# Delta rule and Prelu feed-forward on one core: slopes moved into ScalarE's scale, matmul fillers between the stages of the first chain, conversions dealt out anew

## The chip, the cores and the metric

The kernel runs on one core of a Trainium2 chip. The metric is the device time of one execution in microseconds (us): 669.74, the median of three runs. A core has five engines that run beside each other and meet through semaphores: TensorE (PE, matrix products into the banks of PSUM), VectorE (DVE) and ScalarE (ACT) (elementwise work), GpSimd (POOL), and SyncE (SP), which here issues nearly all the DMA transfers.

## The reference

Two blocks one after the other. The first is the delta rule over 768 time steps for 4 x 8 heads of size 48; the second multiplies the result, as 3072 tokens of 384 numbers, by w_in (384 x 2048), applies a Prelu with a slope per column, and multiplies by w_out (2048 x 384).

```python
k_n = k / (np.linalg.norm(k, axis=-1, keepdims=True) + 1e-06)
for t in range(S):
    kt, vt, bt = (k_n[:, :, t], v[:, :, t], beta[:, :, t, None])
    y[:, :, t] = np.einsum('bhd,bhde->bhe', q[:, :, t], state)
    v_old = np.einsum('bhde,bhd->bhe', state, kt)
    state = state + bt[:, :, :, None] * np.einsum('bhd,bhe->bhde', kt, vt - v_old)
x = y.transpose(0, 2, 1, 3).reshape(B * S, H * D)
h = x @ w_in
g = np.maximum(h, 0.0) + alpha * np.minimum(h, 0.0)
return g @ w_out
```

All data are fp32. alpha lies between 0 and 0.3.

## The kernel before

**Tiling.** Time is cut into 12 chunks of 64 steps (C); a step n of the kernel is one chunk of one pair of batches, so there are 24. Inside a chunk the recurrence becomes triangular algebra: the products of the keys (`grams`, L416) are weighted by beta and the norms (`weigh`, L350), a triangular matrix of 64 x 64 for each head is inverted, first in blocks of 32 (`eliminate`, L499, a long chain of pairs of DVE instructions L514 and L520 with a POOL instruction L504 ahead of it), and the blocks are joined by small products: `between_1` and `between_2` (L671 on PE, with the copies L686 on ACT after each) and `placing` (L624), which puts the inverted blocks, times a mask, into the tile inv. Then `through_state` (L731), `solve` (L762: L765 on PE, L769 on DVE makes u), `outputs` (L774: L778 on PE) and `next_state` (L788: L794 on PE, L802 on DVE) give the chunk's result y and the new state, and `to_ffn` (L810) transposes y on PE (L817) and copies it to xt (L819, ACT) as input of the second block.

**The second block.** `ffn_in` (L899), used for the first 8 chunks, makes 8 pairs of products: for each pair 6 matmuls (L908) fill one of two PSUM banks p_ffn; ACT (L918) writes max(-h, 0) of both halves to SBUF, and DVE adds it, times 1 - alpha, to h (L920, once for each half, as the slope is a number per partition). The bank is free for the next pair but one after L920. `ffn_in_fast` (L1094), for the last 4 chunks, does the same from SBUF: `total` (L1169, DVE), `below` (L1175, ACT), `slope` (L1179, DVE, twice). Their places in time are numbers of PE's steps, kept in a list of due times. `ffn_out` (L938) and its fast forms multiply by w_out.

**Weights.** The two weight matrices come by DMA into staging tiles and are converted, tile by tile, by two ACT instructions (L225, L226) and two DVE instructions (L235, L240): `weights` (L182). One part of a conversion is one of the two DVE instructions; ACT's two are issued up to two tiles ahead. w_in has 12 tiles (24 parts), staged in the space that w_out will take, six at a time: tile 7 can be fetched when tile 1 is converted, and the first w_out tiles that are staged there (four transfers in SP's queue) when the last w_in tiles are. The transfers stand in SP's queue in the order of the program.

**Order of the work.** It is written out by hand; each engine executes its instructions in the order in which the program issues them. `first_chunk` (L1394) is the chain of steps 0 and 1, at the start, when there is no other work for PE. The elimination of its blocks runs on DVE while PE does `busy(BUSY)` (L1531): matmuls of the identity that nobody reads, 512 columns each, here called fillers (L1368; `busy(0.5)` is one of 256 columns). There are two more fillers in the chain, of 0.75 and 0.5. In `first_chunk` the copies and placings of step 1 are on DVE (the arguments `vector` and `by_vector`, L684 and L635), those of step 0 mostly on ACT. 12 parts of the conversion are issued in it, all after `outputs(1)`.

`second_pair` (L1551) does steps 2 and 3 and weaves into them the first chunk's `ffn_in`: `alongside(products, pieces)` issues so many matmuls and so many parts of conversion between two stages. In it the products are dealt out as 4, 5, 4, 4, 5, 5, 5, 5, 5 and the rest, the parts as 2, 2, 2, 2, 3, 3, 3, 2, 2, 1. After it, `ffn_in(1)`, the rest of the conversion, `statics` and the elimination for steps 4 to 7 are woven together (L1622), and from then on attention, elimination and feed-forward run beside each other to the end.

**PSUM.** Three pairs of banks (p_pair) are handed out in turn by `ps_big` and `ps_one` (L76, L81); a filler takes a turn.

## Time and profile before

| what | value |
|---|---|
| median of the three runs | 669.74 us (669.43 to 669.76) |
| profiled execution, its own time | 668.25 us |
| its span, first to last instruction | 666.5 us |
| PE busy, weight loads | 642.7 us (96%), 569.2 us (85%) |
| DVE busy | 494.3 us (74%) |
| ACT busy | 263.1 us (39%) |
| POOL busy | 92.1 us (14%) |
| mean granted clock of PE | 0.984 |
| the chain that ended last, by engine | PE 81%, DVE 11%, ACT 3%, issue 2% |

The profile is one execution, recorded by the hardware. It is read in views: a page of totals; groups of instructions by source line, with count, busy time and mean duration in ns, and after the bar the idle time of the engine just ahead of them and what ended it; windows, which give for stretches of time the busy time of each engine (the number of instructions in brackets), the clock that PE was granted (PEclk, 1.00 is full speed), the busy share of the DMA engines and GB/s; and the timeline, with start, duration, engine, line and operation of each run of instructions, and in square brackets the idle time before it with its releaser. "Issue" as a releaser means that the engine waited for nothing that the profile shows. An fp32 matmul shows as two records. PEld is PE's loading of weights, which overlaps with its products. SPq is SP issuing DMA transfers.

### The profile page before, as it was taken

The numbers are of one execution on the slowest core, as the hardware profiler recorded it, in microseconds if no ns is written. First come the engines' busy times: TensorE is split into PE (matmuls) and PEld (weight loads), VectorE is DVE, ScalarE is ACT, GpSimd is POOL, SyncE is SP. The second block draws the span as 40 slices with busy tenths as digits, with TensorE's granted clock in tenths as the row PEclk, the third lists the DMA queues.
The fourth block names the chain that finished last, engine by engine and source line by source line (L and its number), as shares of the span: only waits on it lengthen the run. The fifth ranks groups of instructions, "written<-read, shape, count | busy, mean of one in ns | idle before, by whom it ended". The sixth has DMA issues, their size and how long they took to land.

```text
span 666.5 us, 22092 instructions
## 1 busy us (share of the span) xinstructions
PE 642.7 (96%) x9535; PEld 569.2 (85%) x9535; DVE 494.3 (74%) x1180; ACT 263.1 (39%) x613; POOL 92.1 (14%) x201
## 2 busy tenths in 40 slices
PE   6979999999999999999999999999999999999997
PEld 4567878656687998998998998998999999999997
DVE  4875879868999859758959757858968658568393
ACT  5736855335455343334343333223235235042140
POOL 6000121001010000001000000000035044052250
PEclk9959999999999999999999999999999999999999
DMA  8848844211432032122112112112112210100000
GB/s 126 230 114 218 197 107 120 71 37 27 77 69 49 12 64 49 22 54 49 25 40 36 24 40 37 24 39 37 26 38 38 37 37 4 28 12 1 25 1 25
DMA packets 110962, 37.72 MB, mean 57 GB/s; under 512 B 104160, under 2 KB 107248, under 8 KB 110864
## 3 DMA queue, kind: packets, MB, share of 16 engines
q1 hardware_dynamic: 109088, 35.81, 25.0%
q8 instruction: 75, 1.23, 0.8%
q10 hardware_dynamic: 1776, 0.49, 0.4%
q14 instruction: 23, 0.19, 0.1%
HBM read 31.56 MB, written 4.72 MB: 54 GB/s over the span
## 4 chain that ended last, share of the span: by engine, by line
PE 81%; DVE 11%; ACT 3%; issue 2%; DMA 1%; POOL 1%; SPq 0%; DVEq 0%; POOLq 0%; ACTq 0%
PE p_ffn L908 21%; PE p_ffn L972 17%; PE p_more L1225 8%; PE p_more L1140 4%; PE p_ffn L1130 3%; PE p_ffn L1225 3%; PE p_pair L375 3%; PE p_pair L671 2%; PE p_ffn L1135 2%; PE p_pair L740 2%; PE p_pair L765 2%; PE p_pair L778 2%; DVE prod L514 2%; PE p_pair L422 2%; DVE block L520 2%
## 5 line engine op out<-in xcount | busy, mean ns | idle before, releaser
L908 PE MATMUL p_ffn<-xt,w_in 128*128 128x256 f32 x768 | 176.3, 385 | 3.8 <-ACT sums L918 1.8
L908 PEld LDWEIGHTS p_ffn<-xt,w_in 128*128 128x128 f32 x768 | 143.8, 191 | 24.6 <-ACT sums L918 2.2
L920 DVE SCALAR_TENSOR_TENSOR act<-act,al_t,p_ffn 128x256 f32<-128x256 f32 x112 | 48.6, 475 | 29.0 <-ACT act L918 28.9
L918 ACT ACTIVATE act<-p_ffn 128x512 f32<-128x512 f32 x56 | 33.3, 594 | 80.9 <-PE p_ffn L908 80.7
L520 DVE TENSOR_TENSOR block<-block,prod 128x30 f32<-128x30 f32 (+9 forms) x150 | 49.9, 333 | 5.1
L1164 POOL TENSOR_TENSOR k_t<-k_t 128x128 f32<-128x128 f32 (+1 forms) x48 | 29.2, 608 | 168.0 <-ACT k_t L1159 165.5
L514 DVE TENSOR_TENSOR prod<-block 128x30 f32<-128x30 f32 (+9 forms) x150 | 48.9, 326 | 3.2 <-POOL block L504 1.6
L972 PE MATMUL p_ffn<-w_out,act 128*128 128x192 f32 x288 | 49.6, 329 | 0.1
L972 PEld LDWEIGHTS p_ffn<-w_out,act 128*128 128x128 f32 x288 | 46.5, 190 | 0.8 <-issue 0.5
L819 ACT COPY xt<-p_pair 128x384 f32<-128x384 f32 x22 | 10.4, 478 | 91.3 <-PE p_pair L817 77.5
L364 POOL TENSOR_TENSOR beta_t<-beta_t,rec 128x8 f32<-128x8 f32 x24 | 6.2, 260 | 290.8 <-DVE rec L362 253.8
L1164 POOL TENSOR_TENSOR block<-block 128x128 f32<-128x128 f32 (+1 forms) x48 | 27.3, 569 | 17.1 <-ACT block L1159 14.6
L1130 PE MATMUL p_ffn<-xt,w_in 128*128 128x256 f32 x96 | 28.8, 381 | 0.5 <-DVE o_sb L992 0.5
L686 ACT COPY inv<-p_pair 32x256 f32<-32x256 f32 x46 | 16.6, 361 | 26.9 <-DVE u L769 23.6
L769 DVE TENSOR_TENSOR u<-p_pair,wgt 128x384 f32<-128x384 f32 x24 | 13.2, 555 | 15.5 <-PE p_pair L671 14.8
L1179 DVE SCALAR_TENSOR_TENSOR act<-block,al_t,act 128x256 f32<-128x256 f32 x32 | 20.3, 675 | 5.3 <-ACT block L1175 5.3
L750 DVE TENSOR_TENSOR r<-v_raw,p_pair 64x192 f32<-64x192 f32 (+1 forms) x66 | 23.3, 353 | 1.1
L992 DVE TENSOR_TENSOR o_sb<-u,p_ffn 128x192 f32<-128x192 f32 x24 | 7.9, 352 | 20.2 <-PE p_ffn L972 19.7
L639 ACT ACTIVATE inv<-inverse,which 128x256 f32<-128x256 f32 x45 | 22.0, 504 | 1.7 <-DVE inverse L487 1.4
L1225 PE MATMUL p_more<-w_out,act 128*128 128x192 f32 x128 | 21.9, 330 | 0.0
L1179 DVE SCALAR_TENSOR_TENSOR act<-k_t,al_t,act 128x256 f32<-128x256 f32 x32 | 21.7, 717 | 0.1
L1159 ACT COPY k_t<-p_more 128x512 f32<-128x512 f32 x16 | 9.4, 585 | 31.4 <-PE p_more L1140 26.7
(223 smaller groups left out, 1398.9 us busy)
## 6 DMA issues: line engine op xcount, KB each, us to landing
w_out<-in_moe_w_in_dram SPq DMA_DIRECT2D x12, 512.0 KB, 6.6
qp<-in_q_dram SPq DMA_DIRECT2D x48, 96.0 KB, 3.3
v_raw<-in_v_dram SPq DMA_DIRECT2D x48, 96.0 KB, 3.0
kl<-in_k_dram SPq DMA_DIRECT2D x96, 48.0 KB, 2.6
out_dram<-o_sb SPq DMA_DIRECT2D x92, 48.0 KB, 1.6
space_out<-in_moe_w_out_dram SPq DMA_DIRECT2D x11, 384.0 KB, 5.1
ke<-in_k_dram SPq DMA_DIRECT2D x43, 96.0 KB, 3.5
w_out<-in_moe_w_out_dram SPq DMA_DIRECT2D x5, 384.0 KB, 5.2
```

Source lines behind the costliest of these rows:

```text
L514: nc.vector.tensor_tensor(out=prod, in0=r[:, 0:j, j : j + 1].to_broadcast([128, j, n]), in1=r[:, j : j + 1, j + 1 : HB].to_broadcast([128, ...
L520: nc.vector.tensor_tensor(out=r[:, 0:j, j + 1 : HB], in0=r[:, 0:j, j + 1 : HB], in1=prod, op=ALU.add)
L750: nc.vector.tensor_tensor(out=r[to, a], in0=v_in[to, a], in1=p[own, a, :, 0:D], op=ALU.subtract)
L908: nc.tensor.matmul(p_h[:, i], w_in[:, t, (f + i) * 128 : (f + i + 1) * 128], xt[:, t], start=(t == 0), stop=(t == KT - 1),)
L918: nc.scalar.activation(g, p_h, ACT.Relu, scale=-1.0)
L920: nc.vector.scalar_tensor_tensor(out=g[:, i], in0=g[:, i], scalar=al_t[:, f + i : f + i + 1], in1=p_h[:, i], op0=ALU.mult, op1=ALU.add,)
L972: nc.tensor.matmul(p, x(i), w(i), start=(i == 0), stop=(i == FP - 1))
L1130: nc.tensor.matmul(p[:, f * 256 : f * 256 + 256], w(2, f), xt[:, 2], start=True, stop=False)
L1140: nc.tensor.matmul(q[:, j], a, b, start=True, stop=True)
L1164: nc.gpsimd.tensor_tensor(out=dst, in0=a, in1=b, op=ALU.add)
L1179: nc.vector.scalar_tensor_tensor(out=g[:, f], in0=r[:, f], scalar=al_t[:, 2 * i + f : 2 * i + f + 1], in1=g[:, f], op0=ALU.mult, op1=ALU.add,)
L1225: nc.tensor.matmul(p, x(i), w(i), start=(i == 0), stop=(i == FP - 1))
```

## The change

The slope moves from DVE to ACT. al_t holds alpha - 1 instead of 1 - alpha, and ACT computes max((alpha - 1) h, 0), with al_t as its scale, once for each half, as the scale is a number per partition; DVE adds h to both halves in one instruction. The same in ffn_in_fast.

In `first_chunk`, there is a filler between all stages, `busy` writes to the pair of banks whose turn is next without taking the turn, step 1's copies and its first placing are on ACT, the placings of part 2 and one scaling of v are on POOL, and the conversion's 12 parts are issued in six portions, the first one ahead of `solve`. BUSY is 7 instead of 6. In `second_pair` the parts are dealt out as 1, 1, 1, 1, 3, 3, 3, 3, 3, 3.

```diff
-BUSY = 6
+BUSY = 7
...
-        nc.scalar.activation(al_t, p, ACT.Copy, scale=-1.0, bias=1.0)
+        nc.scalar.activation(al_t, p, ACT.Copy, bias=-1.0)
...
-            if by_vector:
-                nc.vector.tensor_scalar(
+            if by_pool:
+                nc.gpsimd.tensor_scalar(
...
-                if vector:
+                if both and t == 1:
                     nc.vector.tensor_copy(out=to[rows], in_=p[rows])
...
-    def scale_v(n):
+    def scale_v(n, engine=nc.vector):
...
             g = act_of(c, f // 2)
-            nc.scalar.activation(g, p_h, ACT.Relu, scale=-1.0)
             for i in range(2):
-                nc.vector.scalar_tensor_tensor(
-                    out=g[:, i], in0=g[:, i], scalar=al_t[:, f + i : f + i + 1], in1=p_h[:, i],
-                    op0=ALU.mult, op1=ALU.add,
+                nc.scalar.activation(
+                    g[:, i], p_h[:, i], ACT.Relu, scale=al_t[:, f + i : f + i + 1]
                 )
+            nc.vector.tensor_tensor(out=g, in0=g, in1=p_h, op=ALU.add)
...
             def below():
-                h = g.rearrange("p f i -> p (f i)")
-                nc.scalar.activation(r.rearrange("p f i -> p (f i)"), h, ACT.Relu, scale=-1.0)
+                for f in range(2):
+                    nc.scalar.activation(
+                        r[:, f], g[:, f], ACT.Relu, scale=al_t[:, 2 * i + f : 2 * i + f + 1]
+                    )
 
             def slope():
-                for f in range(2):
-                    nc.vector.scalar_tensor_tensor(
-                        out=g[:, f], in0=r[:, f], scalar=al_t[:, 2 * i + f : 2 * i + f + 1],
-                        in1=g[:, f], op0=ALU.mult, op1=ALU.add,
-                    )
+                nc.vector.tensor_tensor(out=g, in0=r, in1=g, op=ALU.add)
...
-        p = ps_one() if p is None else p
+        p = big[0][:, 0] if p is None else p
...
-        busy(0.75)
+        busy(1)
...
+        busy(0.5)
         for b in range(bs):
             for i in range(4):
                 nc.tensor.matmul(
                     two[quad(i), b], half_way[quad(i), b], inverse[0][quad(i), b, LB:HB]
                 )
+            if b == H - 1:
+                busy(0.5)
         scale_v(0)
...
+        now(between_1(0))
+        place(0, (1,))
+        busy(1)
+        now(between_1(1))
+        place(1, (1,))
+        busy(0.5)
         for i in both:
-            now(between_1(i, vector=i == 1))
-            place(i, (1,), True)
-        place(0, (2,))
-        place(1, (2,), True)
-        scale_v(1)
-        for i in both:
-            now(between_2(i, vector=i == 1))
+            place(i, (2,), True)
+        scale_v(1, nc.gpsimd)
+        now(between_2(0))
         mask(0)
-        for i in both:
-            now(through_state(i))
-            now(solve(i))
+        convert(2)
+        busy(1)
+        now(between_2(1))
         mask(1)
-        busy(0.5)
+        now(through_state(0))
+        now(solve(0))
+        convert(2)
+        busy(0.75)
+        now(through_state(1))
+        now(solve(1))
+        convert(2)
         now(outputs(0))
+        busy(1)
         state_of = [next_state(0)]
         to_ffn(0, ps_ffn())
         now(outputs(1))
+        busy(0.5)
         state_of.append(next_state(1))
-        convert(4)
         to_ffn(1, ps_ffn())
         convert(2)
         for i in both:
             now(state_of[i])
             load_late(i + 2)
             load_v(i + 3)
-        convert(4)
+        convert(2)
...
-        alongside(4, 2)
+        alongside(4, 1)
...
-        alongside(5, 2)
+        alongside(5, 1)
...
-        alongside(5, 2)
+        alongside(5, 3)
...
-        alongside(IN_PARTS - 42, 1)
+        alongside(IN_PARTS - 42, 3)
```

## The prediction, put on record before the changed kernel was run

> **What bounds the kernel now.** I read the windows by stage first, then the clock in windows of half a microsecond, the timeline of the start and of 48 to 105 us, the groups with shapes kept apart, and the order of the instructions of both kernels.
>
> ```profile
> core 0: us, PE busy (x) PEld busy (x) DVE busy (x) ACT busy (x) POOL busy (x), PEclk, DMA share, GB/s
> 27.00:33.00 6.00, 4.91 (x315) 3.75 (x314) 4.94 (x11) 2.31 (x4) 0.00 (x0) 1.00 0.42 74
> 33.00:48.80 15.80, 12.36 (x350) 10.32 (x338) 10.65 (x25) 3.87 (x10) 0.00 (x0) 0.57 0.42 105
> 48.80:100.00 51.20, 47.79 (x1050) 40.40 (x1050) 37.87 (x93) 36.86 (x85) 8.41 (x20) 0.97 0.71 175
> 100.00:146.00 46.00, 44.42 (x292) 31.23 (x292) 38.87 (x111) 19.10 (x42) 3.10 (x8) 1.00 0.31 78
> ...
> 240.00:490.00 250.00, 249.46 (x3613) 228.92 (x3612) 189.04 (x469) 83.03 (x202) 6.58 (x18) 1.00 0.20 38
> 490.00:580.00 90.00, 90.00 (x1411) 86.30 (x1410) 63.13 (x118) 35.88 (x81) 27.90 (x48) 1.00 0.13 25
> ```
>
> From 240 to 580 us PE stands still for 0.54 us. Nothing done to ACT or DVE there can pay; only the start and the stages to about 190 us can move the end. The clock is 0.57 in the first chain (33 to 48.8):
>
> ```profile
> 34.50:35.00 0.50, 0.00 (x0) 0.00 (x0) 0.00 (x0) 0.47 (x2) 0.00 (x0) 0.79 0.53 90
> ...
> 48.00:48.50 0.50, 0.29 (x2) 0.00 (x0) 0.50 (x2) 0.17 (x1) 0.00 (x0) 0.56 0.97 361
> ...
> 65.50:66.00 0.50, 0.50 (x27) 0.50 (x29) 0.50 (x1) 0.49 (x2) 0.44 (x1) 0.51 1.06 424
> ```
>
> The clock falls to half at 34.7 us, recovers at 48.4, and is half again from 65.5 to 68.9. What comes just before the first two falls:
>
> ```profile
> 32.31 1.01 PE L1419 MATMUL p_pair<-inverse,act 32*32 32x16 f32 x82 [0.80 <-issue]
> ...
> 36.32 0.58 PE L671 MATMUL p_pair<-turned,right 32*32 32x32 f32 x15 [2.28 <-issue]
> ...
> 60.85 0.67 ACT L225 ACTIVATE w_in<-w_out 128x512 uint32<-128x512 uint32 x1 [1.81 <-DMA w_out<-in_moe_w_in_dram]
> ...
> 62.72 0.87 DVE L920 SCALAR_TENSOR_TENSOR act<-act,al_t,p_ffn 128x256 f32<-128x256 f32 x2 [3.16 <-ACT act L918]
> ...
> 64.53 0.91 PE L671 MATMUL p_pair<-turned,right 32*32 32x32 f32 x32 [1.51 <-DVE turned L615]
> ```
>
> The waits of 0.80 and 2.28 us end on no engine. Between them PE ran 128 matmuls and 128 weight loads. The page's instruction queue moved 1.23 MB in 75 packets, and all 1.42 MB over 22092 instructions are 64 bytes each: a packet is 256 instructions. I take these waits for late instructions (an inference). The gap of 1.51 us at 63 us has a chain of its own: a late weight tile holds ACT's conversion L225, behind it in order L918, behind that DVE's L920, L240 and L615, and PE needs L615.
>
> [...] 34.72, 48.37, 65.43, 68.85 and 147.3 lie on one grid of 3.41 us. A gap of 1.5 us was enough twice (63.0, 145.2), one of 1.83 at 98.9 not[...] The trace has L918 at 594 ns for 512 elements, the copies L686 at 362 for 256; with a pointer L639 has 504 (from SBUF). [...] L1169 has 685.
>
> ```profile
> L920 DVE SCALAR_TENSOR_TENSOR act<-act,al_t,p_ffn 128x256 f32<-128x256 f32 x112 | 48.6, 475 | 29.0 <-ACT act L918 28.9
> L918 ACT ACTIVATE act<-p_ffn 128x512 f32<-128x512 f32 x56 | 33.3, 594 | 80.9 <-PE p_ffn L908 80.7
> L639 ACT ACTIVATE inv<-inverse,which 128x256 f32<-128x256 f32 x45 | 22.0, 504 | 1.7 <-DVE inverse L487 1.4
> L1179 DVE SCALAR_TENSOR_TENSOR act<-k_t,al_t,act 128x256 f32<-128x256 f32 x32 | 21.7, 717 | 0.1
> L1175 ACT ACTIVATE k_t<-act 128x512 f32<-128x512 f32 x16 | 10.1, 632 | 1.2 <-DVE act L1169 1.1
> L1169 DVE TENSOR_TENSOR act<-p_ffn,block 128x512 f32<-128x512 f32 x12 | 8.2, 685 | 8.2 <-ACT y L729 4.4 <-POOL block L1164 3.8
> ```
>
> **The Prelu.** [...] DVE's two STT, 0.87 us back to back in the timeline, become one TT of 0.69. A pair's bank comes free 0.15 us later when nothing queues; DVE has 0.18 less. In ffn_in_fast, ACT pays 0.95 for 0.63, DVE 0.70 for about 1.39. Over 64 and 32 pairs DVE gets rid of 11.5 + 22 us and ACT gains 21 + 10, but from 240 us on this is covered by PE: taken at 0 (bounds -0.3, +0.6, if 0.15 us more on a bank now and then exceeds its cover, the 2.6 us in which the other bank fills).
>
> **The first chain (PE 27.8 to 48.86).** Work moves: the second chunk's copies and one placing each from DVE to ACT, two placings and one scaling to POOL, mask and conversions up in DVE. POOL has no other work: about 0.8 us each for 256 elements (L1164: 0.78) and 1.1 for 384, done by 37.5 where solve needs them at 40 (bound: twice the price still fits). A full filler costs 0.86 us at full clock (the last of the old ones, two records 0.43 apart), a half one 0.43. With these, on an undropped clock:
> - The seventh filler ends 0.86 later, 28.34; the data were ready at 27.7. First products start 0.57 late, at 28.35, end 29.74.
> - Filler 0.86, then L1408 30.65 to 31.75, filler 0.43, L1417 in two halves of 0.73 with 0.43 between, about 0.2 of late instructions: ends 34.3, addition on DVE 34.8.
> - between_1(0) to 35.0; filler to 35.85; then the next packet. It came 4.0 us after the last in the trace (32.31 to 36.32): 32.9 + 4.0 = 36.9. So 0.95 of the 2.28 us stays. between_1(1) ends 37.5, later than before (36.95).
> - Filler 37.9, between_2(0) 38.6, filler 39.5, between_2(1) 40.15. ACT does both copies in turn, inv1 ready 40.95. solve(0) 40.7, filler 41.35, solve(1) 41.9 (a solve is 0.54 at full clock, 1.1 in the old chain).
> - u(1) waits for a conversion of 1.1 us queued ahead on DVE: 43.05. outputs(0) 42.45, filler 43.3, next_state 43.75, to_ffn 44.2; outputs(1) 44.75, late instructions 0.35, filler 45.5, next_state 46.0, to_ffn 46.4, ACT's copy L819 0.48: first L908 at 47.0.
>
> That is 1.9 us before 48.86. The old chain's steps cost some 4.9 us more at half clock than at full (solves 1.2, betweens 0.8, filler 0.6, outputs, states and transposes 2.4); 3.0 of it go into the fillers, the later start and the order of ACT and DVE.
>
> The fillers now write the pair of banks next in turn and must wait for its last readers; each is done (the tightest: inv0's copies end 39.55, the filler starts 40.7). Behind POOL's three new instructions, which wait for the addition L1424, stands only the weighing at 59 us. The slopes stay one ACT instruction.
>
> **The second pair (48.8 to 101), relative to its start.** Conversions per stretch go from 2,2,2,2,3,3,3,2,2,1 to 1,1,1,1,3,3,3,3,3,3 parts. One conversion fewer lies ahead of L918, and the tiles are requested earlier: the 1.51 us gap and the clock loss after it (1.9 us: L422 1.06 for 0.69, L908 3.68 for 2.15) go. Next late is ACT: mid copies 63.1 to 64.55, ksq, two L919, conversion, then L639 ready at 67.85; PE is there at 66.5 and waits 1.4 us, then 0.65 for the third L639. PE leads by 2.3 at 73.4. But four parts, some 2.2 us of DVE (0.42 + 0.69 a tile), went from a stretch where DVE idled 1.9 and 3.2 us into 73 to 101, where it is nearly full; five TT give back 0.9. I follow DVE: r(3) 79.5, u 84, y 88.5, transposes 92.65, the addition for the eighth pair at 97.1 instead of 96.0, PE waiting 1.6 for its bank; POOL's select and the next addition end 101.75 for 100.64. There PE is 1.0 behind. The four w_out transfers, behind a k load in SP's queue, start near 82.7 for 75.1; ACT's L225 waits some 2.5 us, mostly hidden by DVE (bound: +1).
>
> **To the steady state.** Until 143 the elimination on DVE sets the pace: seven more TT save 1.3, so the chain is back level; PE's gap at 145.2 (1.36) shrinks to 0.2 to 0.4, and the clock window lost at 147.3 (1.7 us) may not be. I credit 0.7 of it, as DVE is full to 190.
>
> **Sum.** -1.9 + 0 - 0.7 = -2.6 us. The profiled execution took 668.25 us (span 666.5, 1.75 around it), giving 665.65; the median lies 1.49 above it and I carry the difference over: 667.1. A measurement of this kernel tells about 0.2%, 1.3 us, from no change.
>
> **Rivals.**
> - *The second pair keeps its lead* (17%): DVE's queue has more slack than I traced, and the 2.3 us survive to the end. For it: removed gap and clock loss, 3.4 us; against: DVE at 0.9 there. 667.1 - 2.3 = 664.8.
> - *Given back* (18%): late DMA adds the 1.0, no clock window is saved at 147 (0.7), and later packets take 0.5 of the start. 669.3; nothing measurable.
> - *The clock drops all the same* (20%): the change doesn't do what it says. The small matmuls may not count as activity. The place is the late packet near 36; it decides if idle time in one 3.41 us window passes about 1.3 us (old falls: 1.48 and 1.5). Then from 38.1, 2.8 us of fillers double and 4.6 of products take half as long again (1.06 for 0.69): +5.1, of which 4.5 show; the chain ends 51.5, 2.6 later than before, 671.6 with 0.7 gained later.
>
> **How the numbers follow.** Forecast 45%, own range 665.6 to 668.4. Faster 0.62, same 0.18, slower 0.20. The range goes to 664.4 below and into the slow case to 671.0 (a drop of one window only, half its price), leaving out about two in ten.
>
> **What would show it.** First L908 near 47.0 and clock 1.00 from 27 to 47; about 1 us of late instructions near 36; no PE wait on L615 near 61, but one on L639; the additions L922 and L1179 near 0.69, L919 near 0.46; PE waits on a bank before 100; nothing new from 240 us. A half clock between 34 and 47, or L919 above 0.55, makes me wrong.

## The result, and the profile after

The changed kernel takes 680.06 us, the median of three runs (679.35 to 680.41), against 669.74: a ratio of 1.0154, with an interval of [1.0131, 1.0177]. It is 10.3 us slower; I had forecast 2.6 us faster. The profiled execution took 679.35 us over a span of 677.6. (Medians, here and below, are of all runs; the intervals of the ratios leave out runs more than 1.5% above the fastest of the same kernel, which are one each of e4 and e9 and three of e12.)

The windows by stage of the changed kernel, cut at its own landmarks (the first L908, that is the end of the first chain, at 54.6 us in place of 48.8); columns: length, busy time of each engine with the number of instructions, clock, DMA share, GB/s:

```profile
27.00:33.00 6.00, 6.00 (x187) 3.33 (x187) 3.71 (x8) 4.00 (x7) 0.00 (x0) 1.00 0.61 106
33.00:54.60 21.60, 19.89 (x496) 12.87 (x490) 9.72 (x21) 5.84 (x15) 3.13 (x3) 0.76 0.39 111
54.60:110.00 55.40, 48.74 (x1042) 40.57 (x1043) 35.38 (x81) 36.58 (x88) 6.47 (x17) 0.92 0.58 140
110.00:156.00 46.00, 45.86 (x298) 32.59 (x298) 38.06 (x106) 21.37 (x50) 4.79 (x12) 0.99 0.31 82
240.00:490.00 250.00, 250.00 (x3689) 229.88 (x3682) 180.06 (x429) 93.77 (x246) 6.58 (x18) 1.00 0.19 38
```

The gaps of the chain are filled, as meant (19.89 busy of 21.60), and yet it ends 5.8 us later than before. The second pair then stands still for 6.7 us of its 55. From 240 on nothing is new. Four landmarks of the two traces give the same picture:

| | before | after | difference |
|---|---|---|---|
| first L908 | 48.86 | 54.65 | +5.8 |
| first L950 / L949 (ffn_out) | 119.8 | 131.8 | +12.0 |
| first L972 / L971 | 215.9 | 226.6 | +10.7 |
| end | 666.5 | 677.6 | +11.1 |

So 5.8 us are lost in the first chain and 6.2 from there to the first `ffn_out`, nearly all of it in the second pair; 1.3 come back from 132 to 227. The timeline of PE in the chain of the changed kernel (start, duration, line, products, and the idle time before them):

```profile
39.06 0.63 PE L671 MATMUL p_pair<-turned,right 32*32 32x32 f32 x28 [1.16 <-issue]
...
41.76 2.08 PE L1365 MATMUL p_pair<-k_t,ident 112*128 112x512 f32 x2
```

and its clock around that place:

```profile
39.00:39.50 0.50, 0.44 (x28) 0.44 (x27) 0.10 (x1) 0.00 (x0) 0.50 (x2) 1.00 0.11 25
39.50:40.00 0.50, 0.50 (x12) 0.46 (x7) 0.00 (x0) 0.27 (x1) 0.50 (x1) 0.61 0.71 131
```

PE stands still for 1.16 us and no engine ends that, which I take for late instructions (I had 0.95); the clock falls at 39.6 and is back only at 49.8: 10.2 us at half speed, in which the two records of a filler take 2.08 us, in place of 1.12 at full clock. The longest waits of PE, apart from that one, from 24 to 110 us, all in the second pair (total, times, longest):

```profile
PE p_ffn L908 <- DVE act L922: 2.5, 1, 2.5
PE p_pair L608 <- issue: 1.5, 1, 1.5
PE p_pair L375 <- ACT inv L686: 1.4, 1, 1.4
PE p_pair L422 <- issue: 1.2, 1, 1.2
```

The clock fell in the pair too, each time for one window of 3.41 us and after a window with one of these waits: at 73.7 (after L422's), at 80.6 (after L375's) and at 107.9 us (after the first). The kernel before lost one such window there (65.5). Stretches inside the three:

```profile
75.00:76.00 1.00, 1.00 (x4) 0.73 (x4) 0.96 (x3) 0.97 (x3) 0.00 (x0) 0.50 0.21 40
82.00:83.00 1.00, 1.00 (x4) 0.82 (x3) 0.52 (x2) 0.41 (x2) 0.17 (x1) 0.50 0.09 16
109.00:110.00 1.00, 1.00 (x4) 0.82 (x3) 0.94 (x3) 0.97 (x4) 0.22 (x1) 0.50 1.20 198
```

The longest wait, 2.5 us up to 108.24, is for the bank that the eighth pair of products had filled. What led to it can be read in the timeline: SP's k load, behind it the w_out transfers, and behind those ACT's conversion L225, which holds up the seventh pair's L919, so that DVE idles for 2.36 us ahead of that pair's L922. With that, DVE's later work is late as well: its transposes L487 and three instructions of conversions (L240, L235, L240) stand ahead of the eighth pair's L922, whose L919 was done at 104.1:

```profile
92.04 1.27 SPq L137 DMA_DIRECT2D ke<-in_k_dram  x2
...
93.42 3.05 SPq L209 DMA_DIRECT2D w_out<-in_moe_w_out_dram  x4
...
97.73 0.58 ACT L225 ACTIVATE w_out<-w_out 128x384 uint32<-128x384 uint32 x1 [3.02 <-DMA w_out<-in_moe_w_out_dram]
100.81 0.81 ACT L919 ACTIVATE act<-p_ffn,al_t 128x256 f32<-128x256 f32 x2
...
101.66 0.69 DVE L922 TENSOR_TENSOR act<-act,p_ffn 128x512 f32<-128x512 f32 x1 [2.36 <-ACT act L919]
...
103.32 0.82 ACT L919 ACTIVATE act<-p_ffn,al_t 128x256 f32<-128x256 f32 x2
...
104.01 2.30 DVE L487 STREAM_TRANSPOSE block<-same 128x256 f32<-128x256 f32 x4 [0.99 <-POOL same L471]
...
107.03 0.56 DVE L240 CUSTOM_DVE_ANT_0 w_out<-w_out 128x768 uint16<-128x768 uint16 x1
107.50 0.68 DVE L922 TENSOR_TENSOR act<-act,p_ffn 128x512 f32<-128x512 f32 x1
```

### The profile page after: what moved, and what is told of

Same layout as the page of the kernel before. It is cut to its first block, busy times and chain, and to the rows that moved or that the text cites. A ratio compares the mean times of both kernels' runs of the same rounds, so it can differ in the third digit from the quotient of the medians.

```text
span 677.6 us, 22105 instructions
## 1 busy us (share of the span) xinstructions
PE 652.1 (96%) x9551; PEld 571.7 (84%) x9551; DVE 465.5 (69%) x1076; ACT 289.2 (43%) x714; POOL 100.1 (15%) x204
## 4 chain that ended last, share of the span: by engine, by line
PE 81%; DVE 9%; ACT 3%; DMA 2%; issue 2%; SPq 1%; POOL 0%; ACTq 0%; POOLq 0%
PE p_ffn L908 21%; PE p_ffn L971 17%; PE p_more L1222 8%; PE p_more L1139 4%; PE p_ffn L1129 3%; PE p_ffn L1222 3%; PE p_pair L1365 3%; PE p_pair L671 3%; PE p_pair L375 2%; PE p_ffn L1134 2%; PE p_pair L765 2%; PE p_pair L740 2%; PE p_pair L778 2%; DVE prod L514 2%; DVE block L520 2%
## 5 line engine op out<-in xcount | busy, mean ns | idle before, releaser
L908 PE MATMUL p_ffn<-xt,w_in 128*128 128x256 f32 x768 | 179.9, 389 | 4.2 <-DVE act L922 3.5
L908 PEld LDWEIGHTS p_ffn<-xt,w_in 128*128 128x128 f32 x768 | 145.8, 194 | 26.1 <-DVE act L922 4.5
L919 ACT ACTIVATE act<-p_ffn,al_t 128x256 f32<-128x256 f32 x112 | 46.8, 468 | 70.6 <-PE p_ffn L908 70.4
L922 DVE TENSOR_TENSOR act<-act,p_ffn 128x512 f32<-128x512 f32 x56 | 38.2, 682 | 37.5 <-ACT act L919 37.3
L1163 POOL TENSOR_TENSOR k_t<-k_t 128x128 f32<-128x128 f32 (+1 forms) x48 | 32.2, 671 | 165.5 <-ACT k_t L1158 163.0
L514 DVE TENSOR_TENSOR prod<-block 128x30 f32<-128x30 f32 (+9 forms) x150 | 48.8, 325 | 3.3 <-POOL block L504 1.6
L971 PE MATMUL p_ffn<-w_out,act 128*128 128x192 f32 x288 | 49.7, 329 | 0.0
L971 PEld LDWEIGHTS p_ffn<-w_out,act 128*128 128x128 f32 x288 | 46.5, 190 | 0.6 <-DVE act L922 0.3
L1163 POOL TENSOR_TENSOR block<-block 128x128 f32<-128x128 f32 (+1 forms) x48 | 29.6, 616 | 14.7 <-ACT block L1158 12.1
L1129 PE MATMUL p_ffn<-xt,w_in 128*128 128x256 f32 x96 | 28.7, 381 | 0.5 <-DVE o_sb L991 0.5
L686 ACT COPY inv<-p_pair 32x256 f32<-32x256 f32 x48 | 17.3, 361 | 25.2 <-DVE u L769 21.4
L639 ACT ACTIVATE inv<-inverse,which 128x256 f32<-128x256 f32 x46 | 22.6, 504 | 1.7 <-DVE inverse L487 1.4
L686 ACT COPY mid<-p_pair 32x256 f32<-32x256 f32 x48 | 17.4, 363 | 12.3 <-PE p_pair L671 9.4
L375 PE MATMUL p_pair<-ident,ke 128*112 128x128 f32 x92 | 15.9, 300 | 6.6 <-POOL ones L267 4.5
L729 ACT COPY y<-p_pair 128x384 f32<-128x384 f32 x22 | 10.4, 478 | 27.4 <-PE p_pair L725 25.3
```

Source lines behind the costliest of these rows:

```text
L375: nc.tensor.transpose(p[0:ROWS, g * 128 : (g + 1) * 128], src[:, 2 * g : 2 * g + 2].rearrange("p h d -> p (h d)")[:, 0:ROWS], ident,)
L514: nc.vector.tensor_tensor(out=prod, in0=r[:, 0:j, j : j + 1].to_broadcast([128, j, n]), in1=r[:, j : j + 1, j + 1 : HB].to_broadcast([128, ...
L686: nc.scalar.copy(to[rows], p[rows])
L908: nc.tensor.matmul(p_h[:, i], w_in[:, t, (f + i) * 128 : (f + i + 1) * 128], xt[:, t], start=(t == 0), stop=(t == KT - 1),)
L919: nc.scalar.activation(g[:, i], p_h[:, i], ACT.Relu, scale=al_t[:, f + i : f + i + 1])
L922: nc.vector.tensor_tensor(out=g, in0=g, in1=p_h, op=ALU.add)
```

## The experiments

Each kernel is compared with the kernel before on the same chip; the table has medians, and the interval of the ratio. They ran on four chips (e1 to e4, e5 to e8, e9 to e12, e13 to e15), on which the kernel before took 669.4 to 670.3 us: a difference between two rows from different chips is uncertain by up to 0.9 us. "Mean clock" is PE's granted clock over a whole run. A value of 0.99 leaves room for 13 us at half speed, so it does not show that one stage kept its clock; a trace shows that, and there is one trace of each kernel.

| run | what it is | us | ratio |
|---|---|---|---|
| e1 | new Prelu alone | 669.06 | [0.9972, 1.0006] |
| e2 | new dealing alone | 672.56 | [1.0024, 1.0055] |
| e3 | new chain alone | 675.91 | [1.0029, 1.0109] |
| e4 | new Prelu and chain | 672.24 | [0.9987, 1.0035] |
| e5 | e4, gaps covered by longer fillers | 669.01 | [0.9979, 1.0021] |
| e6 | e4 without the last five fillers | 666.5 | [0.9930, 0.9975] |
| e7 | the changed kernel, one k load later in SP's queue | 677.35 | [1.0069, 1.0128] |
| e8 | new Prelu and dealing | 671.87 | [1.0012, 1.0035] |
| e9 | e5, fillers over 112 x 32 | 669.09 | [0.9968, 1.0004] |
| e10 | e6 with the new dealing | 671.53 | [1.0012, 1.0048] |
| e11 | e10 with e7's edit | 669.26 | [0.9972, 1.0011] |
| e12 | e5 without its last three fillers | 669.85 | [0.9967, 1.0011] |
| e13 | e5, fillers over 32 x 128 | 683.02 | [1.0171, 1.0210] |
| e14 | e10, four parts after the second pair | 667.9 | [0.9964, 0.9994] |
| e15 | e14 with e7's edit | 668.42 | [0.9974, 1.0028] |

**The parts one by one (e1 to e4, e8).** Each takes over only the functions of one part of the change: `ffn_in` and `below`, `slope` (Prelu), `second_pair` (dealing), `first_chunk` with its helpers (chain).

> The kernel before with the Prelu's new form alone (slope as ACT's scale, one DVE addition). From 226.6 us on the changed kernel takes 451.0 us, the kernel before from the same product 450.6. Theory (the Prelu costs nothing, the loss lies in the chain and the dealing): 669.2 to 670.2. Rival (two ACT instructions with a pointer hold the banks longer, and PE pays for it in the early stages): 672 or more.

> The kernel before with the new dealing of the conversion in the second pair alone (1,1,1,1,3,3,3,3,3,3 parts). Theory A (dealing: conversions move from a stretch where DVE idles to one where it is full, and the w_out transfers come late behind the k load in SP's queue): 672.5 to 675.5, with ACT's L225 waiting about 3 us for w_out and PE waiting for a bank near 100 us. Theory B (the loss after the first chain is only more clock loss and late instructions that follow from the chain's instructions having moved): 669 to 670.5.

> The kernel before with the new first chain alone (fillers, work moved to ACT and POOL, conversions in six portions), old Prelu, old dealing. Theory (the clock drops near 39 us in spite of the fillers, after late instructions, and from then on the fillers cost double): first L908 at 52 to 55 instead of 48.9, total 673 to 676. Rival (the chain lost mostly by the late arrival of alpha's transfer, 17.3 for 15.6 us, which is chance): first L908 near 51, total near 671.

> The changed kernel with the old dealing of the conversion in the second pair. Theory A (dealing costs by itself): 673 to 676.5, so 4 to 6 us less than the changed kernel's 680.1. Theory B (the loss after the chain comes from the chain): 678.5 to 680.5.

> The old first chain with the new Prelu and the new dealing. Prelu alone took 0.9989 of the kernel before, dealing alone 1.0039. Theory A: the dealing's large cost (7.8 us with the other two parts in, 2.3 alone) needs the new first chain, which starts the second pair with other conversions done; then the two simply add: 670.5 to 672 us. Theory B: it needs the new Prelu, whose work on ACT stands ahead of the conversions that the new dealing puts late: then most of the 7.8 us are here too, 675 to 677 us.

e2, e3 and e8 came out within a range that had been named for them; e1 was 0.1 us faster than its theory's, and e4 0.8 faster than theory A's. The Prelu is worth nothing that can be measured. The dealing costs 2.3 us alone, and 2.8 beside the new Prelu (e8 less e1). The chain costs 5.6 alone (seven runs, 668.8 to 678.0; by the interval 1.9 to 7.3). The runs of e4 spread widely, and the mean clock sorts them: at 0.997 four took 665.0 to 667.5 us, at 0.979 to 0.982 seven took 672.3 to 675.4, and the other nine lie between in clock, with 666.7 to 674.1 us. The same instructions thus end some 4 us below e1 or some 4 above it, and the slow runs are those that lost more of the clock. The windows of e4's profiled execution show such a fall at 32.7 us:

```profile
32.00:32.50 0.50, 0.12 (x13) 0.03 (x3) 0.47 (x2) 0.00 (x0) 0.00 (x0) 1.00 0.13 18
32.50:33.00 0.50, 0.44 (x25) 0.41 (x24) 0.09 (x1) 0.00 (x0) 0.00 (x0) 0.73 0.45 85
```

PE had stood still for 0.43 us in the 3.41 us before, a third of what I had named as the limit.

**Fillers that cover the gaps (e5), and no fillers after the fall (e6).**

```diff
 e5, against e4:
         begin_in(6)
-        busy(1)
+        busy(1.5)
...
         place(0, (1,))
-        busy(1)
+        busy(2.5)
         now(between_1(1))
 e6, against e4: busy(0.5), busy(1), busy(0.75), busy(1) and busy(0.5)
 after between_1(1) left out
```

> The new chain and the new Prelu with the old dealing, and two fillers made longer: one and a half in place of one after the first products, two and a half in place of one ahead of the second chunk's products. Without them this kernel took 672.2 us, in single runs 665.0 to 675.4, with a mean clock of 0.997 in the fastest and 0.98 in the slowest. Theory A: the clock falls at the two places where instructions come late (0.43 us among L1417, 1.16 us among L671); 0.43 and 1.29 us more of filler lie just where PE would stand still anyway. The clock is then 1.00 from 27 to 48 us, the first L908 comes at 47.5 to 49, and nearly all runs take 665 to 668 us. Theory B: the small 32 x 32 products do not count as activity, so the clock falls all the same; then the longer fillers only add 0.4 to 2.5 us, and the kernel takes 672.5 to 675 with its first L908 at 54.5 or later.

> The new chain and the new Prelu with the old dealing, without the five fillers after the second chunk's between_1. In the dropped clock these fillers took 1.22, 2.08, 1.65 and some 3 us on PE. Theory A: when the clock is down, it is these fillers at half speed that make the chain late, as some 4 us of theirs lie on its path: first L908 from 54.2 to 49.5 to 51, time 667.5 to 669.5, whether or not the clock holds. Theory B: the chain is late because copies and placings were moved to ACT and POOL (a placing on POOL takes 1.17 us where 0.8 was taken) and conversions lie ahead of its steps: first L908 stays at 53 or later and the time at 671 to 673.

In 17 of e5's 21 runs the clock was 0.99 or more (7 of 20 for e4), and these took 667.7 to 671.9 us; the other four 674 to 675.6. The profile has the clock at 1.00 throughout the chain, and the chain's end at 48.28, inside theory A's 47.5 to 49. The time is not: 669.0 us, where 665 to 668 was expected for nearly all runs. Holding the clock with this much filler gains nothing over the old chain (e1, 669.1). Windows of e5, then the timeline:

```profile
34.00:41.00 7.00, 7.00 (x198) 4.46 (x191) 2.78 (x7) 3.40 (x9) 3.14 (x3) 1.00 0.52 126
41.00:48.00 7.00, 6.72 (x196) 4.40 (x187) 5.16 (x11) 2.22 (x6) 0.00 (x0) 1.00 0.50 144
```

```profile
48.28 1.99 PE L908 MATMUL p_ffn<-xt,w_in 128*128 128x256 f32 x8 [0.57 <-ACT xt L819]
```

e6 gives up on the clock, and is the fastest of all: 666.5 us. Its clock falls all the same, at 33.8, but the chain ends at 47.24 where e4's ends at 54.21, and the clock is back at 44, not 49.8. Windows of e6, then of e4 for the same two stretches:

```profile
34.00:41.00 7.00, 6.30 (x192) 4.54 (x188) 2.78 (x7) 3.22 (x9) 3.14 (x3) 0.50 0.52 127
41.00:48.00 7.00, 6.30 (x202) 5.63 (x201) 5.81 (x12) 3.41 (x8) 0.00 (x0) 0.78 0.37 109
```

```profile
34.00:41.00 7.00, 7.00 (x166) 4.59 (x165) 2.78 (x7) 2.48 (x6) 3.14 (x3) 0.50 0.66 147
41.00:48.00 7.00, 7.00 (x126) 4.26 (x124) 1.79 (x4) 1.45 (x4) 0.00 (x0) 0.50 0.03 6
```

e4 is busy for every microsecond and stays at half clock; e6 has gaps, does 202 products where e4 does 126, and gets the full clock back. The five fillers cost 5.7 us in the median (672.24 less 666.5), and 7.0 in the chain of these two profiles (of which e4's, 673.3 us, is a slower run of its kernel, and e6's, 664.8, a faster one). e6 is better than its theory A had it (first L908 at 49.5 to 51, 667.5 to 669.5 us), and theory B, that ACT's and POOL's new work makes the chain late, falls: e6 has all of that.

**What lets the clock fall (e9, e13).** Neither theory of e5 will do. Theory B, that small products do not count at all, had the clock fall in e5, which kept it. Theory A, that idle time decides, does not fit e6: its clock fell after a window with only 0.19 us of idle time. I weighed each matmul's columns by the share of the array at work, and tested that with fillers of the same length over fewer of its columns (e9), then over fewer of its rows (e13).

```diff
 in busy, within first_chunk; e9:
-                x, ident[0:ROWS], k[0:ROWS, ...]
+                x, ident[0:ROWS, 0:HB], k[0:ROWS, ...]
 e13, into the second bank of the same pair:
-                x, ident[0:ROWS], k[0:ROWS, ...]
+                x, ident[0:HB], k[0:HB, ...]
```

> The kernel with the covered gaps (669.0 us, clock 0.99 to 0.997 in 17 of 21 runs), with the same fillers in the first chain in number, place and length, but each over 112 x 32 of the array in place of 112 x 128. If I weigh each matmul's columns by its share of the array, the 3.41-us windows of the chain held 1465 to 1983 with wide fillers and no fall; in other kernels full-clock windows with 886 to 1031 were followed by a fall although PE stood still for only 0.06 to 0.43 us in them. With narrow fillers the windows come to some 700 to 1100. Theory A: idle time decides: as with wide fillers, 667.5 to 670 us and a clock of 0.99 or more. Theory B: the share of the array at work decides: the clock falls near 31 to 36 us in most runs, the fillers after that take twice the time, first L908 at 53 or later, and the kernel takes 672 to 676 us.

> The kernel with the covered gaps again, with each filler of the first chain over 32 x 128 of the array in place of 112 x 128: a quarter of its rows. With fillers over 112 x 32 (all rows, a quarter of the columns) the time was 669.1 us, 16 of 21 runs with a clock of 0.99 or more, and the clock even came back in a window whose array share, rows by columns, was 0.12. In the profiles so far a matmul's columns weighed by its share of the rows alone sort the windows: under 0.36 of a full window the clock fell after 26 of 28, over 0.54 after none. Theory A (idle time decides): PE is as busy as before, 667 to 670 us with 0.99 or more in three of four runs. Theory B (the share of the rows decides): the windows of the chain come down to some 0.25 to 0.35, the clock falls in nearly all runs and doesn't come back before 48 us: first L908 at 53 or later and 673 to 677 us.

e9 behaves as e5 (16 of 21 runs at 0.99 or more, 669.1 us), so the share of the whole array falls as a theory. e13 has a mean clock of 0.965 to 0.972 in all six runs and took 683 us, even more than theory B's 673 to 677. Idle time falls as a theory too, as the clock stayed at half while PE was busy all the time. Windows of e9, then of e13 (its profiled execution, 687.2 us, is the slowest of the six; the others took 681.2 to 683.6):

```profile
34.00:41.00 7.00, 7.00 (x150) 3.23 (x144) 2.78 (x7) 1.23 (x3) 3.13 (x3) 0.58 0.54 111
41.00:48.00 7.00, 7.00 (x222) 4.05 (x214) 3.08 (x7) 3.16 (x8) 0.00 (x0) 1.00 0.15 42
```

```profile
34.00:41.00 7.00, 7.00 (x109) 3.97 (x104) 2.78 (x7) 1.24 (x3) 3.13 (x3) 0.50 0.50 107
41.00:48.00 7.00, 7.00 (x118) 4.24 (x120) 0.00 (x0) 2.24 (x6) 0.00 (x0) 0.50 0.07 29
```

In both, the clock had fallen near 30 us, after the first products had waited for data (1.30 and 0.92 us). With 112 rows at work in the fillers it came back at 39.8, after three windows; with a quarter of them at 64.2, after ten, in nine of which PE had no gap. (The fillers end with the chain, which here took until 60.6.) What separates the windows of these two traces is the share of the rows that stream, as if a product of 32 rows counted for a quarter of its time. I took, in each 3.41-us window of the 17 profiles up to about 186 us, the sum of columns times rows over 128 (rows in steps of 32; a product counts where it starts), as a share of 4096 columns, which is what eight filler records of 512 columns and 0.43 us fill at full clock. "Fell after" means that the next window is at half clock, "stayed after" that it is still so:

```
share of rows     full clock: fell after    half clock: stayed after
under 0.36              29 of 34                  32 of 32
0.36 to 0.45            14 of 31                  20 of 24
0.45 to 0.54             5 of 25                   6 of 27
over 0.54                0 of 615                  5 of 28
```

By idle time the same full-clock windows mix: of 47 with 0.1 to 0.5 us 5 fell, of 45 with 1 to 1.5 us 14. Columns alone, without a weight for the rows, mix them too: 33 windows fell with over 0.54. The share of the whole array sorts the full-clock windows about as well as the rows do (48 of 64 under 0.36 fell, none of more than 630 over it). What speaks against it is e9 alone: its runs as a whole, and in its trace a half clock that recovered after a window with 0.13 of the array, and a full clock that was kept after one with 0.16. The weights are mine, and some records are missing, so the edge is not sharper than this table. The changed chain's windows have 0.41 and 0.43 (clock kept) and then 0.35 (fell); e4's fell after 0.37, e6's after 0.38; e5's in the chain, from 29 us on, have over 0.54. At half clock fillers do little: the two windows of e4 that are mostly fillers (36.1 to 43.0 us) have 0.31 and 0.32, as a filler's columns then pass at about half the rate (two records took 2.08 us in this trace, 1.12 at full clock). e6, without them, has 0.68 in the window after which its clock returns (40.7 to 44.1), from 64 x 64 products. The new chain was built onto the edge, which fits the spread of its runs, 665 to 675 us; a trace of a run that kept the clock is missing.

**Trimming e5 (e12).**

> The kernel with the covered gaps (669.0 us) without its last three fillers, which lie where 64 x 64 products keep more of the array at work. Theory A: these windows hold the clock by their own products (1940 to 2668 with the fillers, some 1100 to 1500 without), and 0.91 + 1.12 + 0.70 us less stands in the chain, a part of it beside waits: first L908 at 46.5 to 47.5, 666 to 668 us, clock 0.99 or more. Theory B: without the last fillers the clock falls late in the chain, at 42 to 46 us: first L908 at 48 to 50 and 668 to 671 us.

Inconclusive: the median, 669.85, lies in theory B's range, but the runs go from 664.9 to 677.1 us in 21, one of them with a clock of 1.00 and 665.36 us, 12 at 0.99 or more. In its profile, of the slowest run, the first products came 1.61 us late and the clock fell at 30.2 us, before the edit could act.

**The dealing (e7, e10, e11, e14, e15).** e7 moves two `load_early` calls of `second_pair` past the next `alongside`; on SP's queue this takes one k load from ahead of the w_out transfers to behind them, and no other engine's order changes. e14 changes the last parts from 3, 3, 3 to 2, 2, 1 and leaves four to the weaving after the second pair.

```diff
 e7, e11, e15:                                  e14, e15:
-        load_early(x + 2 + NKE)            -        alongside(5, 3)
         now(weigh(x + 2))                  +        alongside(5, 2)
         alongside(5, 3)                     ...
+        load_early(x + 2 + NKE)            -        alongside(5, 3)
 ... and the same for x + 3                 +        alongside(5, 2)
                                             ...
                                            -        alongside(IN_PARTS - 42, 3)
                                            +        alongside(IN_PARTS - 42, 1)
```

> The changed kernel with one edit in SP's queue alone: the k loads of tiles x+2 and x+3 are asked for after the stretch of products that follows them, so that one of them no longer stands ahead of the four w_out transfers. In the changed kernel these transfers started at 93.4 us, behind a k load that waited 9.0 us for PE, and ACT then waited 3.0 and 0.9 us for them. Theory A: this queue is what turns the new dealing's 2.3 us into 7.8: the transfers start near 83, ACT's waits go, the wait of PE for the eighth pair's bank (2.5 us) shrinks below 1 and with it the clock fall at 108; the kernel takes 675 to 677 us. Theory B: DVE's conversions in the full stretch set the pace and the transfers are hidden behind them: 679.5 to 681 us.

> The changed kernel without the five fillers after the second chunk's between_1: new Prelu, new dealing, the other moves of the new chain. With the old dealing the same took 666.5 us (0.9953), and there those fillers cost 5.7 us (672.2 with them). Theory A: the dealing costs its 2.4 us (alone) and more only where the chain ends late with the clock down: 668.5 to 670 us, that is, the five fillers are 10 us of the changed kernel. Theory B: the dealing costs 7.8 us with the moves of the new chain, whether they are late or not: 673.5 to 675 us.

> The same, and one k load of the second pair asked for after the w_out transfers in place of before them, as in the run that took 677.35 in place of 680.06. Theory A: that queue is a part of the dealing's cost here too: 1 to 3 us less than the kernel without it, 666.5 to 668.5. Theory B: the transfers matter only where the chain is late: no difference within 1 us.

> The changed kernel without its last five fillers (671.5 us), and with the last three stretches of the second pair converting 2, 2 and 1 parts in place of 3, 3 and 3: the four parts that are left come after the second pair, beside the blocks' elimination. Theory A: DVE is full in those stretches, so that the four parts are what PE waits for at the eighth pair's bank (2.5 us, with a clock window lost after it): the wait goes back to 1.4 us and the kernel to 668 to 669.5 us. Theory B: the w_out transfers behind a k load are what holds ACT and DVE there (3.8 us of waits), and they stay: 670.5 to 672 us.

> Both mends of the dealing: four parts after the second pair, and one k load behind the w_out transfers (669.3 us with the second alone). Theory A: they take away two different things and add: 666 to 668 us. Theory B: they take away the same wait: no better than 669 us.

The k load in the queue is worth 2.7 us in the changed kernel (e7, five runs, the median 0.35 above theory A's range) and 2.3 on e10 (e11, within theory A's 1 to 3). In e7 the transfers start at 83.6 us in place of 93.4, ACT's waits for them go, PE's wait for the eighth pair's bank shrinks to 0.4 us, and the clock does not fall near 108. SP's timeline of e7:

```profile
81.51 2.00 SPq L137 DMA_DIRECT2D ke<-in_k_dram  x2
83.62 7.38 SPq L209 DMA_DIRECT2D w_out<-in_moe_w_out_dram  x4
```

On the chain without late fillers the dealing costs 5.0 us (e10 less e6), between the two expectations, so neither holds. Taking the four parts out of the full stretch gives 3.6 of them back (e14, just below theory A's range; 3.4 by the ratios to the kernel before on each chip), and PE's wait for the eighth pair's bank, 2.5 us in e10, is gone, and with it the half-clock window that e10 has at 101.0. What is left is a wait for the ninth pair's bank, whose result goes to the tile sums: 1.6 us, much as in e6, which has the old dealing (1.4). PE's longest wait from 85 to 112 us, in e10 and then in e14:

```profile
PE p_ffn L908 <- DVE act L922: 2.5, 1, 2.5
```

```profile
PE p_ffn L908 <- DVE sums L922: 1.6, 1, 1.6
```

ACT still waits 3.2 us for the transfers in e14 (3.8 in e10): with DVE free, that is hidden. The two mends do not add (e15, 668.42, within the spread of e14, between its two theories' ranges). Their traces show why: each takes away the same wait, which is 0.4 us or less in e7, e11, e14 and e15. Why the same dealing costs 2.8 us on the old chain and 5.0 on the new one is open; the profiles of e10 and e8 both have the 2.5 us.

**The sum.** From e1 (669.06): the moves of the chain without its last fillers -2.6 (e6), those fillers +5.7 (e4), the dealing +7.8 (the changed kernel, of which e7 takes 2.7 back): 680. The terms hold in this order alone, as the parts act on each other. A part of the 7.8 is the clock: the changed kernel has 0.975 to 0.985 in its three runs, and against the seven runs of e4 at 0.979 to 0.982 (median 673.9) the dealing costs 6.2.

## Why the prediction was wrong, step by step

1. **The Prelu: right.** 0 was forecast; the medians differ by -1.2, the ratio's interval is -1.9 to +0.4 us (e1). The groups of the changed kernel (line, operation, count, busy time, mean ns of one, idle time before it):

```profile
L919 ACT ACTIVATE act<-p_ffn,al_t 128x256 f32<-128x256 f32 x112 | 46.8, 468 | 70.6 <-PE p_ffn L908 70.4
L922 DVE TENSOR_TENSOR act<-act,p_ffn 128x512 f32<-128x512 f32 x56 | 38.2, 682 | 37.5 <-ACT act L919 37.3
L1179 DVE TENSOR_TENSOR act<-k_t,act 128x512 f32<-128x512 f32 x16 | 13.4, 835 | 1.6 <-ACT k_t L1174 1.6
```

L919 was put at 455 ns, my estimate, on which the 0.15 us more on a bank rests too; it lies between L686's 362 (without a pointer) and L639's 504 (with one), and the trace shows 468. L922 was put at 690, near L1169's 685, and took 682. L1179 is a miss: it takes 835 ns on average (762 from the other buffer) where I took L1169's 685. The trace shows what goes with it: the six of these 32 additions with no POOL instruction beside them took 681 to 693 ns, and of the 26 beside which POOL worked for some of the time, 24 took 727 to 946. DVE saves 0.6 us a pair there, not 0.7; PE covers it.

2. **The first chain: the step that failed.** I wrote that the clock falls "if idle time in one 3.41 us window passes about 1.3 us", an estimate from two falls of the old trace (1.48 and 1.5 us), and reckoned the whole chain "on an undropped clock". On that clock the steps are sound: the first L908 was forecast at 47.0, and e5, with 1.7 us more filler, partly where PE would have waited, has it at 48.28. (The half-clock parts of the old chain add up to 5.0, not 4.9; nothing hangs on it.) The premise is not sound: in the 17 profiles the full clock goes with the rows at work (it fell after 29 of 34 windows with under 0.36 of them, after none of 615 with over 0.54), the products of the chain's first part are 32 x 32, and with its fillers it comes to 0.35 to 0.43 of the rows. The chain was forecast to gain 1.9 us and lost 5.8. The trace of before seemed to speak for idle time: its three falls follow windows with 1.51 to 1.55 us of it, and the gap of 1.83 us at 98.9, which I had named as one that was not enough, is no exception, as a border of the 3.41-us grid (99.6) cuts it into 0.67 and 1.15 us. But it had the counterexample at half clock, which I passed over. From 39 to 47 us, more than two windows, PE had no gap and the clock stayed at half:

```profile
39.00:43.00 4.00, 4.00 (x92) 3.15 (x90) 3.28 (x10) 0.00 (x0) 0.00 (x0) 0.50 0.03 6
43.00:47.00 4.00, 4.00 (x123) 3.58 (x123) 3.60 (x8) 1.28 (x3) 0.00 (x0) 0.50 0.35 113
```

So busy time as the profile counts it did not bring the clock back: here it stayed at 0.50 through 8 us without a gap, in e13 through nine windows of 3.41 us. My rival had the reason in half a sentence ("the small matmuls may not count as activity") and a chance of 20%. Its price was too small, too: the chain's end at 51.5, where 54.65 was measured. I let 2.8 us of fillers double; but fillers at half clock also spread the denser 64 x 64 products that follow, so that the full clock returned after five windows in e4 and after three in e6.

3. **The second pair: the waits foreseen, three sizes off, two clock losses not foreseen.** The gap at 63 us and the clock window behind it went. In their place came waits of PE that no engine ends, for late instructions as I take it (1.54 us at L608 and 1.21 at L422; e4 and e7 have such gaps of 0.9 to 3.1), which I had reckoned with in the chain alone, and the clock was lost at 73.7 and 80.6, which I had not reckoned with at all. The w_out transfers behind the k load, forecast 33.8 us after the first L908, started 38.8 after it (before: 26.2); "mostly hidden by DVE (bound: +1)" was 2.7. And DVE's four parts, which I had at 1.1 us late and a wait of 1.6, made a wait of 2.5 and a clock window lost at 107.9: 3.6 us with what follows (e14; the same wait that e7's edit takes away, so the 2.7 and the 3.6 do not add). I said that the work comes out level; it came out 6.2 us behind. Of the second pair's loss about half is idle time of PE (6.7 us, before 3.4), and the rest is about what two more half-clock windows cost (at most 1.7 us each, half of 3.41).

4. **To the steady state: the clock's 0.7 right, the elimination's 1.3 wrong.** From DVE's first L514 to the end of the gap near 145 (158.5 in the changed kernel) the two traces take 47.1 and 46.9 us: the elimination gained 0.2, not the 1.3 of seven shorter additions. The gap stays at 1.4 us, and is not the 0.2 to 0.4 that I expected. No clock was lost after it, and from there to the next L671 it is 7.0 us in place of 7.7, which is the 0.7 credited. The 1.3 us that come back in all (94.8 in place of 96.1 us from the first L949 to the first L971) are these 0.7 and about half a microsecond after 210.

The range ended at 671.0, as the rival was taken alone: a fall of the clock and a dear dealing were not combined. The 667.1 us forecast was within reach all the same: e6, with the new Prelu and the new chain less its last five fillers, and without the dealing, takes 666.5.

## What to carry to other kernels

Keeping TensorE busy did not keep its clock here: e13's stayed at half through nine windows without a gap. Give a stage of small products fillers that use nearly all the rows (here 112) and bring each 3.41-us window above 0.54 of them (of 615 such windows none was followed by a fall), or leave them out: in the fallen clock a filler's two records took 2.08 us in place of 1.12, and the clock was back after five windows with the fillers (e4) and after three without the last five (e6). Here leaving these five out was the better of the two (666.5 against 669.0 us for e5). Before moving work into a stretch, look at every queue that it passes: here the same edit put DMA requests behind a load that waited for PE. And run a kernel often enough to see whether it stands on such an edge: the same instructions took 665 and 675 us (e4).

## What the runs showed of the hardware that I had not expected

- With fillers over 112 x 32 of the array the clock came back after three windows of 3.41 us, with fillers over 32 x 128 only after ten, when the chain was over (one trace of each; 669.1 and 683.0 us in the median): in these runs rows count, and columns hardly.
- An fp32 addition of 128 x 512 on DVE from SBUF took 681 to 693 ns while POOL stood still and up to 946 while POOL worked beside it.
- Waits of PE that no engine ends, which I take for late instructions, come in more places than the trace of before showed: 0.4 to 3.1 us, at other products in each run. In e4 and in the changed kernel, whose instructions on PE are in the same order up to there, the gap lies exactly 256 records of products and weight loads apart (after 40 of L1417, and after 4 of the second L671): what the prediction took for one packet, and the changed kernel, 2.4 us later at L1417, had missed the first gap.
- A placing on POOL takes 1.17 us for 128 x 256 (2.33 for two, where I took 0.8 from a sum of the same size), but the scaling of 128 x 384 takes 0.82, less than the 1.1 taken.
